# Two 128x2 helpers of a softmax on GpSimd instead of ScalarE

## The chip, the cores and the metric

The kernel runs on one core of one Trainium2 chip. The metric is the device time of one execution in microseconds; the figure before the change is the median of three runs. The core's engines are named as in the profile: PE is TensorE, DVE is VectorE, ACT is ScalarE, POOL is GpSimd, SP is SyncE, which issues most DMAs. PEld is PE's weight load, which overlaps its matmuls.

## The reference

Attention over 4 batches, 8 heads, 768 rows and head size 64, in which a query sees only keys with the same six-bit hash, and then a feed-forward layer over all 3072 rows:

```python
q_bits = (np.einsum('bhsd,dk->bhsk', q, proj) > 0)      # k_bits likewise
mask = q_bucket[:, :, :, None] == k_bucket[:, :, None, :]
scores = scale * np.matmul(q, k.transpose(0, 1, 3, 2))
scores = np.where(mask, scores, -1000000000.0)
scores = scores - np.max(scores, axis=-1, keepdims=True)
attn = np.exp(scores)
attn = attn / (np.sum(attn, axis=-1, keepdims=True) + 1e-09)
out = np.matmul(attn, v)
...
h = x @ w_in                                            # 3072x512 by 512x2048
g = np.where(h > 0.0, h, np.exp(np.minimum(h, 0.0)) - 1.0)
return g @ w_out                                        # 2048x512
```

## The kernel before, in words

All matmuls run in fp16 with every operand split in a high part (hi) and the rest (lo), so that three products of halves give near-fp32 results. Splitting a tile takes two instructions: the high part, mostly on ACT (L142), and scale and subtract, mostly on DVE (L151, one SCALAR_TENSOR_TENSOR that reads the tile and its high part). For the low parts of the weights and of half of the first V tiles, POOL does it in two steps (L153 scales in place, L154 subtracts).

The 3072 rows are cut in eight chunks of 384 (four batches, two each). A chunk has four pairs of heads; a pair of heads has six score rows of 128 queries by 768 keys, called slots here: 24 slots a chunk, 192 in all. What happens in a slot:

- `scores` (L556): four matmuls make a 128x768 score row in PSUM (tile s, or so in every second slot of the opening). DVE's L568 clamps it, copies it to SBUF as pt, and leaves the row maximum in one column of m. This frees the PSUM tile for the next slot.
- After every second slot, `exps` is traced for the two rows (a duo in the code, a pair of score rows in the text): L581 makes nb, the negated and scaled maximum, 128x2; L584 takes the exponential of each row with nb as bias, and leaves the row sum in a column of sm.
- One slot later, `splits`: L593 makes r from sm (scaled, with 1e-9 added), 128x2; DVE's L594 takes the reciprocal; then each row is split in halves (hl, ACT L142 and DVE L151) and transposed by an SP-issued DMA into PT (L599).
- Four slots after the last row of a pair of heads, `attend` multiplies PT with V (L607), and the result is split to x (L616 on ACT, L617 on DVE).

Beside this runs the feed-forward layer of an earlier chunk, 16 tiles of 128 hidden columns a chunk: `h` matmuls (L636), exponential on ACT (L647), `e*up + dn` on POOL (L650), select on DVE (L651), split (ACT L142, DVE L151, tiles U), and two or three tiles later the `o` matmuls (L672). After 16 tiles three output tiles are scaled and written by POOL-issued DMAs (L686).

The opening, up to some 170 us, loads and decodes the weights (L516 on ACT, L517 and L518 on DVE), measures them on PE (L526, tile acc), and splits them (tiles W with scales w0s and w1s), while the first chunk's attention runs. Other names: natk, nat1q and nat2q are split K and Q, zb the hash bits (L320), qm to sg small 128x2 factors, sg holding the scale of the scores and its negative.

A scheduler in the tile framework orders the instructions of each engine by its own estimate of their durations, and sets the semaphores. From slot 30 on (the start of the feed-forward part) PE's order is kept as traced; ACT, DVE, POOL and SP are always ordered by the scheduler. Each engine runs its queue in order.

Of the kernel before, what the change touches and what calls it, by code (L numbers as in the profile page):

```python
# [13 lines left out]
AF = mybir.ActivationFunctionType  # L14
ALU = mybir.AluOpType
# [7 lines left out]
P_TOP = 14  # L23
# [42 lines left out]
def lsh_attention_moe(  # L66
# [10 lines left out]
    nc = tc.nc  # L77
# [60 lines left out]
    def scaled(kind, o, x, s):  # L138

        e = engine(kind)  # L140
        if e == "A":
            nc.scalar.activation(o, x, AF.Copy, scale=s)  # L142
        elif e == "V":
            nc.vector.tensor_scalar(o, x, s, None, ALU.mult)
        else:
            nc.gpsimd.tensor_scalar(o, x, s, 1.0, ALU.mult, ALU.mult)

    def rest(kind, o, x, s, hi):

        if engine(kind) == "V":  # L150
            nc.vector.scalar_tensor_tensor(o, x, s, hi, ALU.mult, ALU.subtract)  # L151
        else:
            nc.gpsimd.tensor_scalar(x, x, s, 1.0, ALU.mult, ALU.mult)  # L153
            nc.gpsimd.tensor_tensor(o, x, hi, ALU.subtract)  # L154
# [421 lines left out]
    def exps(st, duo):  # L576

        m, pts = duo[0], duo[1:]
        w = len(pts)
        nb = small.tile([P, 2], F32, tag="nb", name="nb")  # L580
        nc.scalar.activation(nb[:, :w], m[:, :w], AF.Copy, scale=st["sg"][:, 1:2])  # L581
        sm = small.tile([P, 2], F32, tag="sm", name="sm")
        for n, pt in enumerate(pts):
            nc.scalar.activation(  # L584
                pt, pt, AF.Exp, bias=nb[:, n : n + 1], scale=st["sg"][:, 0:1], accum_out=sm[:, n : n + 1]
            )
        return sm, pts

    def splits(sm, pts, PTs):

        w = len(pts)
        r = small.tile([P, 2], F32, tag="r", name="r")
        nc.scalar.activation(r[:, :w], sm[:, :w], AF.Copy, scale=2.0**-P_TOP, bias=1e-9 * 2.0**-P_TOP)  # L593
        nc.vector.reciprocal(r[:, :w], r[:, :w])  # L594
        for n, pt in enumerate(pts):
            hl = pp.tile([P, 2, S], F16, tag="p", name="hl")
            scaled("p_hi", hl[:, 0, :], pt, r[:, n : n + 1])
            rest("p_lo", hl[:, 1, :], pt, r[:, n : n + 1], hl[:, 0, :])
            nc.sync.dma_start_transpose(PTs[n].rearrange("p x c e -> p (x c) e"), hl.rearrange("p x e -> p (x e)"))  # L599
# [189 lines left out]
    for ns in groups:  # L789
# [3 lines left out]
        for n in ns:  # L793
            at = lead[2] if early else begin[n] - PREP[2]

            w = 2 * chunks[pairs[n][0]]["nc"]
# [144 lines left out]
    def run_splits():  # L941
        if behind:
            splits(*behind.pop())

    for G in range(starts[-2] + 1):
        if G == starts[0]:
            ordered.enter_context(tc.manual_schedule(engines={mybir.EngineType.PE}))
        if G < len(slots):
            n, at = slots[G]
            c = chunks[pairs[n][0]]  # L950
            b, p, j, t = c["b"], pairs[n][1], at // c["nc"], at % c["nc"]
            now[0] = int(w_at == NSI + NSO)
            if t == 0:
                (PT,) = pt_ring.take(c["nc"], pairs[n][0])
                PTs = PTs + [PT] if j else [PT]
            if G < starts[0] and G % 2:
                s_tile = ps_o.tile([P, 2, 512], F32, tag="o", name="so")
            else:
                s_tile = ps_s.tile([P, 2, 512], F32, tag="s", name="s")
            scores(ks[b, p], qs[n], at, j, s_tile, duo, G >= starts[0])  # L960
            into.append(PT[:, t])

            run_splits()
            if len(into) == 2:
                behind.append((*exps(qs[n], duo), into))
                duo, into = [], []
            if at == 2 * c["nc"] - 1:
                assert not into
                waiting.append((G + AV_LAG, (n, PTs)))
        else:  # L970
            run_splits()
# [39 lines left out]
```

## Time and profile before

| | |
|---|---|
| median of three runs | 927.86 us (924.74 to 927.88) |
| the profiled execution | 925.77 us, span of its instructions 923.3 us |
| mean granted PE clock | 0.938 of full speed |
| busy: PE, DVE, ACT, POOL | 823.7, 698.3, 696.0, 221.9 us |
| PE busy, 0 to 184 us / 184 to 876 us | 109.2 / 675.1 us |

The page cuts the span in 40 slices; a digit is a busy share in tenths (9 is 90% or more), and PEclk the granted clock in tenths.

```profile
PE   4475745899999999999989999999999999999996
DVE  6999968788878778788868687889878687674332
ACT  7876878989869677789879677888687777774322
POOL 1703579631112011212211111221111112111211
PEclk9577656899999999999999999999999999999998
```

The first eight slices are the opening, in which PE has gaps and a lower granted clock. From the ninth on PE is nearly always busy, and in the last four no attention is left.

A row of a group has the line, engine and operation, the output and inputs, shapes and count, then the busy time and the mean in ns of one, and then the idle time before and what ended it. A row of the timeline has its start and its duration in us. A row of waits has who waited for whom, the total in us, the count and the longest.

### The profile page before, as it was taken

The numbers are of one execution on the slowest core, as the hardware profiler recorded it, in microseconds if no ns is written. First come the engines' busy times: TensorE is split into PE (matmuls) and PEld (weight loads), VectorE is DVE, ScalarE is ACT, GpSimd is POOL, SyncE is SP. The second block draws the span as 40 slices with busy tenths as digits, with TensorE's granted clock in tenths as the row PEclk, the third lists the DMA queues.
The fourth block names the chain that finished last, engine by engine and source line by source line (L and its number), as shares of the span: only waits on it lengthen the run. The fifth ranks groups of instructions, "written<-read, shape, count | busy, mean of one in ns | idle before, by whom it ended". The sixth has DMA issues, their size and how long they took to land.

```text
span 923.3 us, 14935 instructions
## 1 busy us (share of the span) xinstructions
PE 823.7 (89%) x5161; PEld 434.4 (47%) x5161; DVE 698.3 (76%) x1490; ACT 696.0 (75%) x1361; POOL 221.9 (24%) x259
## 2 busy tenths in 40 slices
PE   4475745899999999999989999999999999999996
PEld 2232312455545555555545555555445555555553
DVE  6999968788878778788868687889878687674332
ACT  7876878989869677789879677888687777774322
POOL 1703579631112011212211111221111112111211
PEclk9577656899999999999999999999999999999998
DMA  9799576798787857698897776896876678554000
GB/s 327 202 282 254 143 148 128 138 170 174 154 177 160 144 111 142 146 191 141 154 216 130 129 127 120 165 192 110 158 140 130 118 118 151 100 108 84 35 1 34
DMA packets 391338, 135.11 MB, mean 146 GB/s; under 512 B 368000, under 2 KB 385632, under 8 KB 391264
## 3 DMA queue, kind: packets, MB, share of 16 engines
q1 hardware_dynamic: 389184, 127.88, 69.3%
q0 software_dynamic: 1920, 6.29, 2.0%
q8 instruction: 40, 0.66, 0.3%
q14 instruction: 34, 0.28, 0.1%
q10 hardware_dynamic: 160, 0.00, 0.0%
HBM read 35.65 MB, written 6.29 MB: 45 GB/s over the span
## 4 chain that ended last, share of the span: by engine, by line
PE 45%; DVE 19%; DMA 13%; ACT 12%; issue 8%; POOL 1%; SPq 1%; ACTq 0%; POOLq 0%; DVEq 0%
PE h L636 16%; PE o L672 15%; PE s L556 7%; PE av L607 6%; DVE pt L568 5%; DVE hl L151 4%; DMA K<-natk 4%; ACT pt L584 3%; DMA O<-nat1q 3%; ACT hl L142 3%; DMA PT<-hl 2%; DMA out_dram<-W 2%; DVE W L518 1%; ACT U L647 1%; PE z L315 1%
## 5 line engine op out<-in xcount | busy, mean ns | idle before, releaser
L672 PE MATMUL o<-W,U 128*128 128x512 f16 x1152 | 280.9, 380 | 2.4 <-ACT W L142 2.4
L636 PE MATMUL h<-x,W 128*128 128x384 f16 x1536 | 280.5, 327 | 2.6 <-DVE x L617 2.2
L650 POOL TENSOR_SCALAR U<-U,ch 128x384 f32<-128x384 f32 x128 | 113.4, 886 | 572.1 <-ACT U L647 506.0
L636 PEld LDWEIGHTS <-W 128*128 128x128 f16 x1536 | 147.5, 98 | 114.1 <-issue 10.7
L151 DVE SCALAR_TENSOR_TENSOR hl<-pt,r,hl 128x768 f16<-128x768 f32 x192 | 193.9, 1038 | 6.3 <-ACT hl L142 5.9
L584 ACT ACTIVATE pt<-pt,nb,sg 128x768 f32<-128x768 f32 x192 | 195.3, 1018 | 2.2
L142 ACT ACTIVATE hl<-pt,r 128x768 f16<-128x768 f32 x192 | 168.4, 925 | 29.8 <-DVE r L594 27.6
L568 DVE TENSOR_SCALAR_CACHE_REDUCE pt<-s 128x768 f32<-128x768 f32 x177 | 168.0, 949 | 25.1 <-PE s L556 24.4
L556 PE MATMUL s<-K,O 128*128 128x384 f16 x708 | 151.5, 337 | 22.7 <-DVE pt L568 19.8
L672 PEld LDWEIGHTS <-U 128*128 128x128 f16 x1152 | 111.1, 98 | 122.3 <-issue 8.8
L556 PEld LDWEIGHTS <-O 128*128 128x128 f16 (+1 forms) x768 | 74.8, 102 | 115.6 <-issue 59.2
L651 DVE SCALAR_TENSOR_TENSOR U<-h,U 128x384 f32<-128x384 f32 x128 | 70.8, 553 | 74.8 <-POOL U L650 74.7
L647 ACT ACTIVATE U<-h,ch 128x384 f32<-128x384 f32 x128 | 72.8, 569 | 66.2 <-PE h L636 66.1
L607 PE MATMUL av<-PT,vhl 128*64 128x384 f16 x1152 | 106.9, 332 | 3.8 <-DMA PT<-hl 3.7
L151 DVE SCALAR_TENSOR_TENSOR U<-U,ch 128x384 f16<-128x384 f32 x128 | 79.6, 623 | 39.7 <-ACT U L142 39.4
L142 ACT ACTIVATE U<-U,ch 128x384 f16<-128x384 f32 x128 | 77.2, 605 | 40.8 <-DVE U L651 40.5
L607 PEld LDWEIGHTS <-vhl 128*64 128x64 f16 x1152 | 68.8, 111 | 44.4 <-issue 15.4
L154 POOL TENSOR_TENSOR W<-W 128x512 f16<-128x512 f32 x32 | 43.5, 1363 | 2.2
L581 ACT ACTIVATE nb<-m,sg 128x2 f32<-128x2 f32 x96 | 27.5, 287 | 16.4 <-DVE pt L568 15.9
L584 ACT ACTIVATION_READ_ACCUMULATOR pt<-pt,nb,sg 128x1 f32 x192 | 36.0, 187 | 0.0
L526 PE MATMUL acc<-W 128*128 128x128 bf16 x128 | 17.8, 283 | 19.7 <-DVE W L518 19.2
L556 PE MATMUL so<-K,O 128*128 128x384 f16 (+1 forms) x60 | 18.7, 449 | 17.9 <-DVE pt L568 16.6
(126 smaller groups left out, 632.5 us busy)
## 6 DMA issues: line engine op xcount, KB each, us to landing
U<-in_moe_w_in_dram SPq DMA_DIRECT2D x12, 512.0 KB
vf<-in_v_dram SPq DMA_DIRECT2D x16, 384.0 KB
U<-in_moe_w_out_dram SPq DMA_DIRECT2D x12, 512.0 KB
out_dram<-W POOLq DMA_DIRECT2D x24, 256.0 KB, 3.4
qst<-in_q_dram SPq DMA_DIRECT2D x30, 192.0 KB
kst<-in_k_dram SPq DMA_DIRECT2D x14, 384.0 KB
PT<-hl SPq DMA_TRANSPOSE x192
W<-in_moe_w_in_dram SPq DMA_DIRECT2D x4, 512.0 KB
```

The lines of the kernel that those rows point to most:

```text
L142: nc.scalar.activation(o, x, AF.Copy, scale=s)
L151: nc.vector.scalar_tensor_tensor(o, x, s, hi, ALU.mult, ALU.subtract)
L154: nc.gpsimd.tensor_tensor(o, x, hi, ALU.subtract)
L556: nc.tensor.matmul(s_tile[:, n, :HALF], st[o][:rows, at, :], kst[kk][:rows, j * NC + n * HC : j * NC + (n + 1) * HC, :].rearrange("p a b - ...
L568: top = nc.vector.tensor_scalar(pt.rearrange("p (n e) -> p n e", n=2), s_tile[:, :, :HALF], CLAMP, None, ALU.max, ALU.max, accum_out=duo[0 ...
L584: nc.scalar.activation(pt, pt, AF.Exp, bias=nb[:, n : n + 1], scale=st["sg"][:, 0:1], accum_out=sm[:, n : n + 1])
L607: nc.tensor.matmul(av[j * D : (j + 1) * D], vt[:, j, c, vx, :], PTs[j][:, :, px, c, :], start=n == 0, stop=n == last,)
L636: nc.tensor.matmul(h, WH[:, g * KT + t, wx, fc * P : (fc + 1) * P], c["xs"][t][:, xx, :], start=n == 0, stop=n == 3 * KT - 1,)
L647: nc.scalar.activation(e, h, AF.Exp, scale=c["ch"])
L650: nc.gpsimd.tensor_scalar(e, e, c["up"], c["dn"], ALU.mult, ALU.add)
L651: nc.vector.scalar_tensor_tensor(e, h, 0.0, e, ALU.max, ALU.min)
L672: nc.tensor.matmul(o[t][:, :DO], g16[:, gx, t * P : (t + 1) * P], WH[:, NSI + 1 + f, wx, :], start=f == 0 and i == 0, stop=f == NF - 1 and ...
```

## The change

L581 and L593, the two 128x2 instructions between the row maxima and the exponentials and between the row sums and the reciprocal, are issued on POOL instead of ACT. nb reads one operand per partition (sg) and an immediate 1.0; r has two immediates. Nothing else is edited; the scheduler orders the changed program anew.

```diff
         nb = small.tile([P, 2], F32, tag="nb", name="nb")
-        nc.scalar.activation(nb[:, :w], m[:, :w], AF.Copy, scale=st["sg"][:, 1:2])
+        nc.gpsimd.tensor_scalar(nb[:, :w], m[:, :w], st["sg"][:, 1:2], 1.0, ALU.mult, ALU.mult)
...
         r = small.tile([P, 2], F32, tag="r", name="r")
-        nc.scalar.activation(r[:, :w], sm[:, :w], AF.Copy, scale=2.0**-P_TOP, bias=1e-9 * 2.0**-P_TOP)
+        nc.gpsimd.tensor_scalar(r[:, :w], sm[:, :w], 2.0**-P_TOP, 1e-9 * 2.0**-P_TOP, ALU.mult, ALU.add)
         nc.vector.reciprocal(r[:, :w], r[:, :w])
```

Three places of the new order are shown in the prediction: POOL between two output DMAs, where 96 nb and 96 r now stand among the 128 L650; DVE behind a row maximum; and POOL among the weight splits of the opening.

## The prediction

> **What bounds the kernel now.** I read the page's busy shares first, then busy time by stretch, then the waits of PE, and last single rows in order of time. The columns of the second view are the stretch, its length, busy time of PE, PE's weight loads, DVE, ACT and POOL, then granted PE clock, DMA share and GB/s.
>
> ```profile
> PE 823.7 (89%) x5161; PEld 434.4 (47%) x5161; DVE 698.3 (76%) x1490; ACT 696.0 (75%) x1361; POOL 221.9 (24%) x259
> 23.00:115.00 92.00, 57.28 (x347) 29.46 (x346) 89.56 (x199) 73.02 (x137) 38.10 (x30) 0.65 0.85 221
> 115.00:184.00 69.00, 42.64 (x229) 19.64 (x229) 51.90 (x93) 59.07 (x116) 53.11 (x51) 0.70 0.73 138
> 184.00:876.00 692.00, 675.07 (x4318) 359.82 (x4317) 529.87 (x1124) 534.07 (x1055) 120.01 (x141) 1.00 0.74 140
> ```
>
> There are two kernels in one. From 184 us on, PE is busy 675.07 of 692.00 us, and only 16.9 us can be won there. Before that no engine is full all the time: DVE has 97% of 23 to 115 us, and from 115 to 184 us ACT has 86%, POOL 77%, DVE 75%. POOL does 91 of its 222 us between 23 and 184 us; later it is busy 17%.
>
> What PE still waits for after 184 us:
>
> ```profile
> PE s L556 <- DVE pt L568: 10.5, 10, 2.3
> PE o L672 <- ACT W L142: 2.4, 4, 1.2
> PE av L607 <- DMA PT<-hl: 2.4, 4, 1.1
> ```
>
> The largest wait is for the row maximum (L568), which empties the one score tile in PSUM. So a delay counts there only when it makes a later L568 late, or the transposed probabilities (PT).
>
> **The change, part by part.** *Removed from ACT:* 96 of each instruction (the third and fourth row are the stretches up to 167 and from 23 to 115 us).
>
> ```profile
> L581 ACT ACTIVATE nb<-m,sg 128x2 f32<-128x2 f32 x96 | 27.5, 287 | 16.4 <-DVE pt L568 15.9
> L593 ACT ACTIVATE r<-sm 128x2 f32<-128x2 f32 x96 | 18.3, 190 | 0.2
> L581 ACT ACTIVATE nb<-m,sg x14: 278/281/297, 24.4 to 162.2; 128x2 f32<-128x2 f32 x14
> L581 ACT ACTIVATE nb<-m,sg x8: 278/281/297, 24.4 to 106.8; 128x2 f32<-128x2 f32 x8
> 50.98 0.28 ACT L581 ACTIVATE nb<-m,sg 128x2 f32<-128x2 f32 x1
> 51.17 0.65 ACT L516 ACTIVATE W<-W 128x512 f32<-128x512 f32 x1
> 90.61 0.19 ACT L593 ACTIVATE r<-sm 128x2 f32<-128x2 f32 x1
> 90.70 0.66 ACT L516 ACTIVATE W<-U 128x512 f32<-128x512 f32 x1
> ```
>
> Busy time is 27.5 + 18.3 = 45.8 us, but the next instruction starts 0.19 us after an nb and 0.09 us after an r, since neighbours overlap. ACT really gets back 0.28 us per pair of score rows: 27 us over 96 pairs. 14 pairs lie before 167 us (3.9 us), 82 after it. Before 115 us DVE is the full engine, so I count half of the 3.9: −2 us. Behind 184 us ACT is busy 77% and PE's waits name it with 2.4 us: −1 us.
>
> *Added on POOL, busy time:* no 128x2 TENSOR_SCALAR runs on POOL before the change, so its price comes from the shortest of wider ones (columns: min/median/max in ns) and, as a floor, from a memset of one column.
>
> ```profile
> L153 POOL TENSOR_SCALAR vf<-vf,vs x8: 582/945/1532, 29.2 to 42.9; 128x384 f32<-128x384 f32 x8
> L153 POOL TENSOR_SCALAR W<-W,w1s x16: 687/698/1659, 115.0 to 188.2; 128x512 f32<-128x512 f32 x16
> L650 POOL TENSOR_SCALAR U<-U,ch x128: 652/666/2766, 172.9 to 910.4; 128x384 f32<-128x384 f32 x128
> L237 POOL MEMSET pjt<- 32x1 f32 x8 | 0.5, 91 | 0.2
> ```
>
> 128 more columns cost 105 ns, 0.82 ns each, so 384 columns are 315 ns and the fixed part is 267 ns with one operand read per partition (nb's form). L650 reads two and has 337 ns, so one such operand is 70 ns, and r, with none, would be near 197 ns. The sum is 0.46 us per pair, 45 us in all. The low end is 0.18 us (two memsets of 91 ns), the high end 1.33 us (two of L650's median, as if width cost nothing); I take 0.46, worked out from the same kind of instruction. Behind 184 us POOL has 572 us idle, which hides it; if POOL were full, those 82 pairs would cost 38 us.
>
> *Hops.* Here is one pair in the steady part, in order of time.
>
> ```profile
> 307.84 1.01 DVE L151 SCALAR_TENSOR_TENSOR hl<-pt,r,hl 128x768 f16<-128x768 f32 x1
> 307.96 0.29 ACT L581 ACTIVATE nb<-m,sg 128x2 f32<-128x2 f32 x1 [0.63 <-DVE pt L568]
> 308.28 1.03 ACT L584 ACTIVATE pt<-pt,nb,sg 128x768 f32<-128x768 f32 x1
> 308.77 0.61 DVE L151 SCALAR_TENSOR_TENSOR U<-U,ch 128x384 f16<-128x384 f32 x1
> 310.32 0.56 ACT L647 ACTIVATE U<-h,ch 128x384 f32<-128x384 f32 x1
> 310.98 0.67 POOL L650 TENSOR_SCALAR U<-U,ch 128x384 f32<-128x384 f32 x1 [5.49 <-ACT r L593]
> 311.68 0.56 DVE L651 SCALAR_TENSOR_TENSOR U<-h,U 128x384 f32<-128x384 f32 x1 [0.51 <-POOL U L650]
> 312.27 0.61 ACT L142 ACTIVATE U<-U,ch 128x384 f16<-128x384 f32 x1 [1.30 <-DVE U L651]
> 312.92 0.62 DVE L151 SCALAR_TENSOR_TENSOR U<-U,ch 128x384 f16<-128x384 f32 x1 [0.68 <-ACT U L142]
> 313.45 0.95 DVE L568 TENSOR_SCALAR_CACHE_REDUCE pt<-s 128x768 f32<-128x768 f32 x1
> 314.33 0.08 DVE L568 DVE_READ_ACCUMULATOR pt<-s 128x1 f32 x1
> 315.17 0.82 PE L556 MATMUL s<-K,O 128*128 128x384 f16 x4
> ```
>
> L647 ends at 310.88 and POOL starts at 310.98: a hop to POOL is 0.10 us. POOL ends at 311.65, DVE starts at 311.68: 0.03 us back. Undisturbed, nb costs 0.10 + 0.27 + 0.03 = 0.40 us on its path against 308.28 − 307.92 = 0.36 us now, and r about 0.10 us more than now. By that the move would be nearly free in latency.
>
> *Disturbance by DVE.* It isn't undisturbed. This L650 fell into a run of DVE's L151:
>
> ```profile
> 257.82 1.94 DVE L151 SCALAR_TENSOR_TENSOR hl<-pt,r,hl 128x768 f16<-128x768 f32 x2
> 257.99 2.76 POOL L650 TENSOR_SCALAR U<-U,ch 128x384 f32<-128x384 f32 x1 [4.57 <-ACT U L647]
> 259.68 0.60 DVE L151 SCALAR_TENSOR_TENSOR U<-U,ch 128x384 f16<-128x384 f32 x1
> ```
>
> It took 2.76 us where the median is 0.67, and ended 0.47 us after the third L151. L151 reads two tensors from SBUF. So POOL stands still until a run of them is over. The Trainium skill says why: in "SBUF — State Buffer", section "SBUF: two separate sides", the port pair that DVE and GpSimd share is an exclusive lock, taken for a whole instruction by a DVE operation with two SBUF inputs or by a GpSimd one, and the other blocks. The row agrees; by that rule nothing of such a wait is shared or shortened, and the sum below would stand at its upper end for every nb that meets one.
>
> How often does nb meet it? It is released by the second L568 of a pair, so what DVE has in its queue right behind that decides. In the changed order that is an L151 in 41 of 96 pairs. DVE in the fourth of eight chunks, before (pt is the score row, m its maximum, hl the split probabilities, U a feed-forward tile, natk the split K, zb the hash bits):
>
> ```order
> L151 SCALAR_TENSOR_TENSOR natk<-kst,ks,natk 128x768
> L568 TENSOR_SCALAR pt,m<-s 128x768
> L651 SCALAR_TENSOR_TENSOR U<-h,U 128x384
> L151 SCALAR_TENSOR_TENSOR hl<-pt,r,hl 128x768
> L320 TENSOR_SCALAR zb<-z,pjt 64x384
> L151 SCALAR_TENSOR_TENSOR hl<-pt,r,hl 128x768
> ```
>
> and DVE at the same place now:
>
> ```order
> L151 SCALAR_TENSOR_TENSOR natk<-kst,ks,natk 128x768
> L568 TENSOR_SCALAR pt,m<-s 128x768
> L151 SCALAR_TENSOR_TENSOR hl<-pt,r,hl 128x768 x2
> L320 TENSOR_SCALAR zb<-z,pjt 64x384
> L651 SCALAR_TENSOR_TENSOR U<-h,U 128x384
> ```
>
> The two hl splits moved ahead of L651, straight behind the maximum that releases nb. One L151 holds POOL for 1.01 us, two for 1.94; 1.2 us is my mean.
>
> In the pair quoted above L151 starts at 307.84, nb could start at 307.92 + 0.10 = 308.02 at the earliest and would wait for both L151, until 309.38. With its 0.27 and the hop, the exponentials (L584) would start at 309.68 instead of 308.28, 1.4 us late. L647 follows them on ACT, L650, L651, the next U split and then L568 follow that one by one, each released by the last or nearly so; L568 would end 1.4 us later than 314.41, at 315.8, where PE wants the tile at 315.17. PE loses 0.6 us. Where ACT has idle time between, it loses nothing. Blocked pairs in the steady part: 82 × 41/96 = 35. At 0.6 us each this is 21 us, the upper end; the lower is 0. I let somewhat under half of it through: +9 us. In the opening 14 × 41/96 = 6 pairs are blocked; 1.2 us each, half of it kept because ACT is idle 14 to 21% there: +3 us (0 to 7).
>
> *What queues behind on POOL.* POOL is in order, so L650 and the weight splits now stand behind an nb that waits for DVE and an r that waits for ACT. POOL in the steady part, before:
>
> ```order
> L650 TENSOR_SCALAR U<-U,ch 128x384 x15
> L686 DMA out_dram<-W 128x512 x2
> L650 TENSOR_SCALAR U<-U,ch 128x384
> L686 DMA out_dram<-W 128x512
> L650 TENSOR_SCALAR U<-U,ch 128x384 x15
> ```
>
> and now, behind the second chunk's output:
>
> ```order
> L650 TENSOR_SCALAR U<-U,ch 128x384
> L686 DMA out_dram<-W 128x512
> L581 TENSOR_SCALAR nb<-m,sg 128x2
> L650 TENSOR_SCALAR U<-U,ch 128x384
> L593 TENSOR_SCALAR r<-sm 128x2
> ```
>
> Where fifteen L650 followed each other, an nb or an r now stands between two of them. DVE's L651 waits for L650, PE's o matmuls come two feed-forward tiles later, and PE waits only 2.4 us for all outputs: I cost this at nothing there. The cover is that lag of two tiles; if it is gone, each late L650 stops PE's o matmul. SP's queue loses and gains no DMA.
>
> *DVE held by POOL.* It goes the other way too: of the 192 L151 of this form the median took 1010 ns and the longest 1904.
>
> ```profile
> L151 DVE SCALAR_TENSOR_TENSOR hl<-pt,r,hl x192: 998/1010/1904, 34.8 to 839.0; 128x768 f16<-128x768 f32 x192
> ```
>
> On the full DVE of 23 to 115 us some 8 pairs × 0.46 = 3.7 us is the most that small POOL operations can take; they must start first to do so: +1 us.
>
> Sum: −2 − 1 + 9 + 3 + 1 = +10 us. The profiled execution took 925.77 us (span 923.3), so 935.8, told as 936. It lies 2.1 us under the median of the runs, 927.86.
>
> **Rivals.** *ACT's time is worth more (faster).* The freed 27 us shorten ACT's queue, hl and U splits come earlier, L568 is never late. For it: undisturbed latency is the same within 0.1 us, and most L650 run at 0.67 us. Against it: only 17 us of PE waits exist behind 184 us and ACT is not full there. The whole 3.9 us of the opening and half of the 10.5 us on L568 go: 925.77 − 9 = 917. It decides if nb's mean stays below about 0.5 us.
>
> *All hidden (no change).* Blocked nb are covered by ACT's 23% idle time, the freed 0.28 us pays for the rest: 926 to 930. For it: PE is 97.6% busy and loses only 2.4 us to PT today. Against it: the pair above, where every step followed at once.
>
> *POOL and ACT chain each other in the opening (much slower).* From 115 to 184 us POOL is busy 77% with weight splits, and ACT's next high part overwrites what POOL's low part reads. There POOL has, before (w0s and w1s are the scales of the two weights):
>
> ```order
> L153 TENSOR_SCALAR W<-W,w1s 128x512
> L154 TENSOR_TENSOR W<-W 128x512
> L153 TENSOR_SCALAR W<-W,w0s 128x512
> L153 TENSOR_SCALAR W<-W,w1s 128x512
> L154 TENSOR_TENSOR W<-W 128x512 x2
> ```
>
> and now:
>
> ```order
> L153 TENSOR_SCALAR W<-W,w1s 128x512
> L581 TENSOR_SCALAR nb<-m,sg 128x2
> L154 TENSOR_TENSOR W<-W 128x512
> L153 TENSOR_SCALAR W<-W,w0s 128x512
> L154 TENSOR_TENSOR W<-W 128x512
> L593 TENSOR_SCALAR r<-sm 128x2
> ```
>
> The scaling (L153) and the subtraction (L154) of one weight tile are parted by an nb, and an r that waits for exponentials holds the next tile. 14 − 8 = 6 pairs, two holds each, each as long as one row's exponentials (1.03 + 0.19 us): +15 us on the forecast, 951. Against it: ACT waits little for POOL there now:
>
> ```profile
> ACT W L142 <- POOL W L154: 1.2, 4, 0.6
> ```
>
> **How the numbers follow.** Something under 0.5% (4.6 us) can't be told from no change. Blocked nb, as summed: 0.45, of which 0.41 beyond 932.5 us and 0.04 within; its own range is 929 to 950, from the nb terms' ends. All hidden: 0.28. ACT's time worth more: 0.15. The chain in the opening: 0.12. So faster 0.15, same 0.32, slower 0.53. The range leaves out the better half of the faster case (0.08) and, at the top, the chain with longer holds (some 0.06): 922 to 955.
>
> **What would show it.** Right: nb on POOL with a median near 0.3 us but a mean above 0.6 and a maximum above 1.5; DVE's and ACT's idle time in the steady part up; PE's wait for L568 behind 184 us above 10.5 us, towards 20; the first feed-forward matmul (L636) later than the 166.91 us of this row:
>
> ```profile
> 166.91 1.63 PE L636 MATMUL h<-x,W 128*128 128x384 f16 x9
> ```
>
> Wrong: nb's mean below 0.5 us, or PE's waits unchanged despite long nb (the 9 us fall away), or an opening that ends earlier because the changed order of ACT and DVE there happens to fit better, which I can't price from the trace.

## The result and the profile after

The changed kernel takes 939.35 us (median of four runs, 935.04 to 943.29) against 926.30 of the kernel before, timed beside it on the same chip: 1.0139 times as long, 95% interval 1.0117 to 1.0161, or 13 us. The profiled execution took 937.45 us, with a span of 935.7; before it was 925.77 and 923.3.

Busy time over the whole span, from the page:

```profile
PE 828.0 (88%) x5161; PEld 434.7 (46%) x5161; DVE 703.1 (75%) x1490; ACT 663.3 (71%) x1169; POOL 293.0 (31%) x451
```

And the three stretches of before (stretch, length, busy us of PE, PE's weight loads, DVE, ACT and POOL, granted PE clock, DMA share, GB/s):

```profile
23.00:115.00 92.00, 50.59 (x305) 26.18 (x305) 85.70 (x188) 70.42 (x119) 41.05 (x44) 0.63 0.82 222
115.00:184.00 69.00, 47.29 (x245) 22.58 (x244) 49.04 (x96) 53.30 (x93) 58.25 (x63) 0.71 0.71 128
184.00:876.00 692.00, 668.71 (x4275) 353.68 (x4276) 539.21 (x1128) 507.38 (x902) 181.13 (x303) 1.00 0.74 141
```

ACT has 33 us less to do and POOL 71 us more, yet PE does 6.4 us less of its work between 184 and 876 us (668.71 against 675.07). Besides PE (97%) no engine is full: DVE is busy 78% there, ACT 73%, POOL 26%. So the loss is to be looked for in waits. PE's, from 184 us on (who waited for whom, total us, count, longest):

```profile
PE s L556 <- DVE pt L568: 17.1, 16, 2.5
PE av L607 <- DMA PT<-hl: 2.1, 3, 0.9
```

The wait for the row maximum grew from 10.5 to 17.1 us; the one for the transposed probabilities did not. One engine further back, the groups of the moved instructions and their neighbours (busy us, mean ns of one | idle before it and what ended it):

```profile
L581 POOL TENSOR_SCALAR nb<-m,sg 128x2 f32<-128x2 f32 x96 | 56.0, 583 | 235.5 <-DVE pt L568 159.0 <-DVE qm L187 31.9 <-DVE qs L200 21.4
L593 POOL TENSOR_SCALAR r<-sm 128x2 f32<-128x2 f32 x96 | 22.4, 233 | 159.7 <-ACT pt L584 158.7
L584 ACT ACTIVATE pt<-pt,nb,sg 128x768 f32<-128x768 f32 x192 | 195.4, 1019 | 79.3 <-POOL nb L581 79.0
```

The same wait by the view of waits, ACT from 190 to 900 us:

```profile
ACT pt L584 <- POOL nb L581: 71.4, 61, 3.2
```

The exponentials are as long as before (1019 ns against 1018), but ACT, whose queue is in order, now stands idle 79.0 us in front of them. In the kernel before it stood 16.4 us in front of its own nb, as quoted in the prediction. So ACT lost more to waiting than the 45.8 us of busy time it was relieved of. Part of such a wait is for the maximum itself: counting only the time between the end of a pair's second maximum and its first exponential, over the 81 pairs behind the opening, ACT is idle 56.4 us now and was 11.3 us before. How long nb and r take, minimum, median and maximum in ns:

```profile
L581 POOL TENSOR_SCALAR nb<-m,sg x96: 254/267/2298, 25.3 to 845.4; 128x2 f32<-128x2 f32 x96
L593 POOL TENSOR_SCALAR r<-sm x96: 181/191/1482, 28.0 to 847.9; 128x2 f32<-128x2 f32 x96
```

The medians are small. The mean of nb is more than twice its median, since a third of them are stretched. One of these, from the opening, with the rows of DVE around it in order of time:

```profile
158.83 1.01 DVE L151 SCALAR_TENSOR_TENSOR hl<-pt,r,hl 128x768 f16<-128x768 f32 x1
...
159.00 1.42 POOL L581 TENSOR_SCALAR nb<-m,sg 128x2 f32<-128x2 f32 x1 [0.49 <-DVE pt L568]
...
159.76 0.60 DVE L151 SCALAR_TENSOR_TENSOR nat2q<-qst,qs,nat1q 128x384 f16<-128x384 f32 x1
...
160.46 1.03 ACT L584 ACTIVATE pt<-pt,nb,sg 128x768 f32<-128x768 f32 x1 [3.12 <-POOL nb L581]
```

nb is released at 159.00, but two L151 run until 160.36, and it ends 0.06 us after them; the exponential starts 0.04 us later. ACT had been idle for 3.12 us, about half of it before the maximum was there. The first feed-forward matmul comes 3.9 us later than before:

```profile
170.81 2.44 PE L636 MATMUL h<-x,W 128*128 128x384 f16 x14
```

### The profile page after: what moved, and what is told of

Its sections match the earlier page's. It is cut to its first block, busy times and chain, and to the rows that moved or that the text cites. A ratio compares the mean times of both kernels' runs of the same rounds, so it can differ in the third digit from the quotient of the medians.

```text
span 935.7 us, 15092 instructions
## 1 busy us (share of the span) xinstructions
PE 828.0 (88%) x5161; PEld 434.7 (46%) x5161; DVE 703.1 (75%) x1490; ACT 663.3 (71%) x1169; POOL 293.0 (31%) x451
## 5 line engine op out<-in xcount | busy, mean ns | idle before, releaser
L636 PE MATMUL h<-x,W 128*128 128x384 f16 x1536 | 281.0, 327 | 0.0
L584 ACT ACTIVATE pt<-pt,nb,sg 128x768 f32<-128x768 f32 x192 | 195.4, 1019 | 79.3 <-POOL nb L581 79.0
L151 DVE SCALAR_TENSOR_TENSOR hl<-pt,r,hl 128x768 f16<-128x768 f32 x192 | 195.1, 1047 | 9.0 <-ACT hl L142 8.7
L636 PEld LDWEIGHTS <-W 128*128 128x128 f16 x1536 | 147.8, 98 | 111.7 <-issue 10.9
L568 DVE TENSOR_SCALAR_CACHE_REDUCE pt<-s 128x768 f32<-128x768 f32 x177 | 168.3, 951 | 16.0 <-PE s L556 15.0
L650 POOL TENSOR_SCALAR U<-U,ch 128x384 f32<-128x384 f32 x128 | 112.3, 878 | 202.1 <-ACT U L647 190.8
L581 POOL TENSOR_SCALAR nb<-m,sg 128x2 f32<-128x2 f32 x96 | 56.0, 583 | 235.5 <-DVE pt L568 159.0
L607 PE MATMUL av<-PT,vhl 128*64 128x384 f16 x1152 | 108.8, 339 | 6.4 <-DMA PT<-hl 5.6
L151 DVE SCALAR_TENSOR_TENSOR U<-U,ch 128x384 f16<-128x384 f32 x128 | 79.6, 622 | 21.6 <-ACT U L142 19.5
L593 POOL TENSOR_SCALAR r<-sm 128x2 f32<-128x2 f32 x96 | 22.4, 233 | 159.7 <-ACT pt L584 158.7
L594 DVE RECIPROCAL r<-r 128x2 f32<-128x2 f32 x96 | 15.7, 163 | 59.0 <-POOL r L593 58.7
```

Of the source, the lines that this page charges most:

```text
L568: top = nc.vector.tensor_scalar(pt.rearrange("p (n e) -> p n e", n=2), s_tile[:, :, :HALF], CLAMP, None, ALU.max, ALU.max, accum_out=duo[0 ...
L581: nc.gpsimd.tensor_scalar(nb[:, :w], m[:, :w], st["sg"][:, 1:2], 1.0, ALU.mult, ALU.mult)
L584: nc.scalar.activation(pt, pt, AF.Exp, bias=nb[:, n : n + 1], scale=st["sg"][:, 0:1], accum_out=sm[:, n : n + 1])
L607: nc.tensor.matmul(av[j * D : (j + 1) * D], vt[:, j, c, vx, :], PTs[j][:, :, px, c, :], start=n == 0, stop=n == last,)
L636: nc.tensor.matmul(h, WH[:, g * KT + t, wx, fc * P : (fc + 1) * P], c["xs"][t][:, xx, :], start=n == 0, stop=n == 3 * KT - 1,)
L650: nc.gpsimd.tensor_scalar(e, e, c["up"], c["dn"], ALU.mult, ALU.add)
```

## The experiments

Each kernel was timed against the kernel before on the same chip, whose medians lay between 924.83 and 925.60 us (926.30 for the change itself). Where us are given as a gain or loss, they are differences of the medians of one chip. The right part of the table is from the profiled executions: how much later than before the 43rd and the last of the 192 slots started (the L568 rows in order; the 43rd starts at 219.5 us before), how long ACT was held up for nb between 190 and 900 us, and the median time from the end of a pair's second row maximum to the start of its first exponential, over the 81 pairs behind the opening.

| | median us | ratio, 95% interval | slot 43 | slot 192 | ACT idle for nb, us | max to exp, median us |
|---|---|---|---|---|---|---|
| before | | 1 | | | 15.0 | 0.58 |
| the change | 939.35 | 1.0139 (1.0117 to 1.0161) | +8.9 | +12.6 | 71.4 | 1.10 |
| nb alone on POOL | 940.94 | 1.0169 (1.0151 to 1.0187) | +3.1 | +16.4 | 64.8 | 1.10 |
| r alone on POOL | 927.34 | 1.0023 (1.0012 to 1.0033) | +5.6 | +1.8 | 30.4 | 0.51 |
| both on POOL, opening only | 930.25 | 1.0051 (1.0033 to 1.0068) | +5.9 | +5.0 | 14.5 | 0.60 |
| both on POOL, from slot 30 on | 935.72 | 1.0114 (1.0095 to 1.0132) | +5.1 | +10.3 | 72.4 | 1.10 |
| both on DVE | 933.27 | 1.0081 (1.0061 to 1.0101) | +2.8 | +8.4 | 51.0 | 1.63 |
| nb alone on DVE | 934.11 | 1.0093 (1.0079 to 1.0106) | +4.0 | +9.3 | 38.9 | 1.66 |
| both on ACT, unused copies on POOL | 932.79 | 1.0080 (1.0062 to 1.0098) | +6.7 | +7.0 | 15.7 | 0.65 |
| nb on POOL in two steps | 961.35 | 1.0386 (1.0367 to 1.0405) | +11.7 | +37.5 | 82.6 | 1.69 |
| nb on ACT in two steps | 942.18 | 1.0165 (1.0143 to 1.0186) | +6.5 | +16.8 | 9.3 | 1.33 |
| unused copy of sm on ACT | 928.51 | 1.0033 (1.0011 to 1.0055) | −0.6 | +1.2 | 14.4 | 0.73 |

The start of slot 43 scatters by a few us from kernel to kernel, and no run separates why, so single numbers of that column carry little; the growth from slot 43 to slot 192 is steadier. That growth goes with the last column: the seven kernels in which the median is above 1 us lose between 3.7 and 25.8 us behind slot 43, the four others at most 1.8. Its size does not follow the median: nb alone on DVE, at 1.66 us, loses 5.3 there, and nb in two steps on POOL, at 1.69, loses 25.8. ACT's idle time for nb alone is no measure of the loss either: with r alone on POOL it is twice that of before, and with nb on ACT in two steps it is less.

**Which of the two.** nb alone on POOL:

```diff
-        nc.scalar.activation(nb[:, :w], m[:, :w], AF.Copy, scale=st["sg"][:, 1:2])
+        nc.gpsimd.tensor_scalar(nb[:, :w], m[:, :w], st["sg"][:, 1:2], 1.0, ALU.mult, ALU.mult)
```

> Only nb (L581) goes to POOL; r stays on ACT. Whole change: +1.39% (+13 us). Theory A, nb blocked behind DVE's L151 makes the exponentials late: most of it returns, +8 to +12 us, nb's mean near 0.58 us and its maximum above 2 us, ACT waiting some 70 us for nb. Theory B, POOL's queue and the two-way chain with ACT in the opening: nb and r share it, +4 to +8 us. Theory C, the scheduler's new order of ACT and DVE: anything from -5 to +13 us, with no relation to nb's duration.

And r alone:

```diff
-        nc.scalar.activation(r[:, :w], sm[:, :w], AF.Copy, scale=2.0**-P_TOP, bias=1e-9 * 2.0**-P_TOP)
+        nc.gpsimd.tensor_scalar(r[:, :w], sm[:, :w], 2.0**-P_TOP, 1e-9 * 2.0**-P_TOP, ALU.mult, ALU.add)
```

> Only r (L593) goes to POOL; nb stays on ACT. Theory A: r is released by ACT, not by DVE's row maximum, so it seldom meets a run of L151; mean near 0.23 us, and the time is within 3 us of before. Theory B: +4 to +8 us, since r holds the weight splits on POOL until the exponentials are done. Theory C: anything from -5 to +13 us.

nb alone costs 15.5 us, all that the change costs and a little more; r alone 1.9 us. With nb on POOL the lag grows from +3.1 us at slot 43 to +16.4 at the end; with r it shrinks. r's wait is behind the exponentials and one slot ahead of the split that uses it. nb's stands between the row maximum and the exponentials, with ACT waiting. The 15.5 us lie above all three ranges, 3.5 us above theory A's; its other signs came (nb's mean is 609 ns, ACT idle for nb 64.8 us). For r, theory A's range of 3 us held. PE's waits with nb alone on POOL, from 184 us on, show a second way of the loss: beside the row maximum, PE now waits for the transposed probabilities, which cost it 2.4 us before.

```profile
PE s L556 <- DVE pt L568: 17.4, 18, 2.7
PE av L607 <- DMA PT<-hl: 8.9, 9, 1.8
```

The pair of kernels also bears on theory C, the new order. If the instructions of ACT and DVE are matched by operation and tiles, without the moved helpers, then r alone has 188 of ACT's 913 and 375 of DVE's 1298 out of the order of before (the fewest that would have to be moved back), the whole change 181 and 365, and nb alone 129 and 190. As much re-ordering as in the change comes with 1.9 us, less of it with 15.5. So the amount of re-ordering is not what costs; that one particular order does is not excluded by this.

**Which part of the run.** The two new lines are chosen by a flag that is set at slot 30 (here the opening; the other kernel has the branches exchanged):

```diff
-        nc.scalar.activation(nb[:, :w], m[:, :w], AF.Copy, scale=st["sg"][:, 1:2])
+        if not late[0]:
+            nc.gpsimd.tensor_scalar(nb[:, :w], m[:, :w], st["sg"][:, 1:2], 1.0, ALU.mult, ALU.mult)
+        else:
+            nc.scalar.activation(nb[:, :w], m[:, :w], AF.Copy, scale=st["sg"][:, 1:2])
...
+        late[0] = int(G >= starts[0])
```

> nb and r on POOL only for the pairs of score rows before slot 30, on ACT after it. In the profile after, slot 30 began 5.2 us and slot 42 8.9 us later than before, the last slots 12.6 us later. Theory A: the opening has 15 pairs, some 6 blocked, +3 to +5 us at slot 30 and no more after it. Theory B: +8 to +10 us, all of it by slot 42. Theory C: the opening's order is that of the changed kernel, so slot 30 is late by the same 5 us whatever POOL does.

> nb and r on POOL only from slot 30 on, on ACT before it. Theory A: 81 pairs, some 35 blocked: +5 to +9 us, spread evenly over the slots, with PE's wait for L568 after 184 us at 15 to 18 us. Theory B: the weight splits still run until slot 36 or so: +2 to +5 us, all of it between slots 30 and 42. Theory C: with the opening as before, -3 to +5 us.

+4.8 us for the opening, +10.3 for the steady part; together 15.0 against 13.0 for the whole change, within the intervals. The opening's loss is complete by slot 43 and does not grow; at slot 31 it is 4.3 us, which fits theories A and C alike. The steady part's loss is not spread evenly, as theory A had it: 5.1 of the 10.3 us are there by slot 43, 3.6 of them from slot 31 on, where theory B had its loss; the other 5.2 come behind it. PE's wait for L568 is 16.6 us, within theory A's 15 to 18. The changed kernel itself has lost 5.2 us by slot 31, 8.9 by slot 43, and 3.7 us behind that.

**Without POOL.** If the block of POOL by L151 were all of it, nb on DVE would be nearly free:

```diff
-        nc.scalar.activation(nb[:, :w], m[:, :w], AF.Copy, scale=st["sg"][:, 1:2])
+        nc.vector.tensor_scalar(nb[:, :w], m[:, :w], st["sg"][:, 1:2], None, ALU.mult)
```

> nb and r go to DVE instead of POOL: ACT is freed by the same instructions, but nothing stands on POOL and nothing has to wait there. nb only on POOL cost +1.69% (15.6 us), all of it after slot 30. Theory A, the wait of nb for a run of L151 and the late exponentials behind it: without POOL the loss is gone, 920 to 928 us (DVE pays some 0.15 us for each, of which a few us may show in the opening, where DVE is full). Theory C, the order that the scheduler makes when ACT has less to do: the loss stays, 934 to 942 us. Theory D, the load taken off ACT and put elsewhere is what counts: ACT had 77% and DVE 77% in the steady part, so the time stays within 3 us of before.

> Only nb goes to DVE, r stays on ACT. Theory A: 920 to 928 us, against 941 with nb on POOL. Theory C: 934 us or more. If both this and the kernel with both on DVE are faster than before, nb's place is what the gain belongs to.

Theory A missed on both: 933.27 and 934.11 us, not 920 to 928. Theory C's 934 or more, for the order of the scheduler, is met with nb alone and missed by 0.7 us with both. With nb alone on DVE it is short (min/median/max in ns):

```profile
L581 DVE TENSOR_SCALAR nb<-m,sg x96: 210/223/1203, 25.6 to 842.0; 128x2 f32<-128x2 f32 x96
```

And yet ACT waits for it, here by the view of waits from 190 to 900 us:

```profile
ACT pt L584 <- DVE nb L581: 38.9, 39, 1.8
```

In the order of that kernel an L151 stands straight ahead of nb on DVE in 61 of the 96 pairs. So there nb waits in DVE's queue for the same kind of instruction that held it on POOL. The delay has another cause and the same place, and the kernel loses 8.5 us. These two kernels do not part lateness from order: that an L151 stands ahead of nb is itself the scheduler's order.

**Without the path.** nb and r are made on ACT as before, and POOL makes both a second time into tiles that nobody reads:

```diff
+        nbx = small.tile([P, 2], F32, tag="nx", name="nbx", bufs=1)
+        nc.gpsimd.tensor_scalar(nbx[:, :w], m[:, :w], st["sg"][:, 1:2], 1.0, ALU.mult, ALU.mult)
...
+        rx = small.tile([P, 2], F32, tag="nx", name="rx", bufs=1)
+        nc.gpsimd.tensor_scalar(rx[:, :w], sm[:, :w], 2.0**-P_TOP, 1e-9 * 2.0**-P_TOP, ALU.mult, ALU.add)
```

> nb and r stay on ACT and are used from there; POOL makes the same two 128x2 results a second time, into a tile that nobody reads. Theory A: nobody waits for these, so 0 to +4 us, although they last as long on POOL as in the changed kernel. Theory B, POOL's queue (L650 and the weight splits behind waiting instructions) and DVE held by POOL: the same +6 to +13 us as the change.

It loses 7.2 us, above theory A's 4 and within theory B's 6 to 13, all of it by slot 43. Behind that, POOL has the same small instructions in its queue, stretched the same way, and nothing is lost. Their group, with a mean of 591 ns:

```profile
L583 POOL TENSOR_SCALAR nbx<-m,sg 128x2 f32<-128x2 f32 x96 | 56.7, 591 | 185.1 <-DVE pt L568 108.3 <-DVE qm L187 41.5 <-DVE qs L200 21.5
```

In the opening ACT waits for POOL's low parts of the weights (0 to 190 us). It was 1.2 us in the kernel before; in this one it is:

```profile
ACT W L142 <- POOL W L154: 6.0, 6, 2.2
```

In the changed kernel that wait is 4.9 us, with both on POOL in the opening only 6.4. It is of the size of the opening's loss. Order has little part in it here: counted as above, only 17 instructions of ACT and 11 of DVE stand elsewhere than before, all between 133 and 195 us. The lag grows from 1.0 us at slot 29 (161 us) to 6.5 at slot 34 (182 us), while POOL splits weights. So a loss as large as the opening's arises without a late nb; how it divides between POOL's queue, DVE held by POOL and the few moved instructions is open.

**The dose.** nb alone on POOL, with a second instruction behind it:

```diff
+        nc.gpsimd.tensor_scalar(nb[:, :w], nb[:, :w], 1.0, 1.0, ALU.mult, ALU.mult)
```

> As nb only on POOL (940.9 us), and a second 128x2 instruction on POOL multiplies nb by 1 before ACT may use it: some 0.2 to 0.3 us more on the path of each pair, and a second chance to meet an L151. Theory A, the time follows nb's lateness (0.3 us more on average cost 15.6 us): +5 to +15 us on top, 946 to 956 us. Theory C, order alone: within 4 us of 941.

The group of that second instruction:

```profile
L582 POOL TENSOR_SCALAR nb<-nb 128x2 f32<-128x2 f32 x96 | 49.1, 511 | 6.7
```

PE's wait for the row maximum, 184 to 930 us:

```profile
PE s L556 <- DVE pt L568: 31.3, 31, 2.0
```

49.1 us more between maximum and exponentials cost 20.3 us more than nb alone on POOL (35.8 against 15.5), and PE's wait is three times that of before. Of the lag added to that of nb alone, 8.6 us are there by slot 43 and 12.5 follow over the rest. The direction is theory A's; its range ended at 15 us, and 961.35 lies 5 us above it.

**One operand of L151 in PSUM.** To see whether the two SBUF inputs of L151 are what holds POOL, the high part that DVE's splits subtract was replaced by a zero in PSUM:

```diff
+    av_bank = ps_a.tile([P, 512], F32, tag="av", name="av")
+    zero_ps = av_bank[:, 448:452]
...
-            nc.vector.scalar_tensor_tensor(o, x, s, hi, ALU.mult, ALU.subtract)
+            nc.vector.scalar_tensor_tensor(o, x, s, z, ALU.mult, ALU.subtract)
```

where z is one column of zero_ps, repeated, and av takes the rest of the same bank. The second kernel has nb on POOL besides.

> The kernel before (nb and r on ACT) with one operand of every DVE split of the form L151 taken from PSUM instead of SBUF: the high part that is subtracted is replaced by a zero in an unused corner of the PSUM bank of av. It leaves out the subtraction of the high part, and keeps the wait for it. It is the base for the next run, and has its own order of DVE. Theory lock (POOL stands still while DVE reads two operands from SBUF): POOL's L650 no longer stretches, maximum below 1.2 us where it was 2.77, and the time is 915 to 930. Theory order (an engine other than ACT makes nb late by its place in a queue, the lock is a small part): L650's maximum may fall as well, the time is 920 to 935. If L650 still stretches past 2 us, two operands in SBUF are not what holds POOL.

> The run above with nb alone on POOL. It too leaves out the subtraction of the high part. To be compared with the run above, as nb alone on POOL (940.94) is with the kernel before (925.47), +15.5 us. Theory lock: nb has a mean of 0.27 to 0.32 us and no instance above 0.7, and the difference falls to +4 us or less. Theory order: nb is as short as that, but ACT still waits 40 us or more for it, and the difference stays at +8 us or more, as when nb ran on DVE (+8.6).

The times were 1364.62 and 1387.42 us (ratios 1.4733, 1.4701 to 1.4765, and 1.4975, 1.4933 to 1.5018), far from both expectations. Since av and the zero share a tile, the matmuls that write to this tile wait until DVE has read the zero. PE's largest such wait in the first kernel, from 190 us on:

```profile
PE av L329 <- DVE U L161: 155.9, 38, 8.8
```

The difference between the two, 22.8 us, is as theory order had it (8 or more), and so is ACT's idle time for nb, 54.1 us; but in the first kernel, with nb on ACT, that time is already 49.3 us. The difference is one of a kernel that waits elsewhere, and it decides nothing about the time. The durations do decide something. L151 is line 161 here, L650 line 664 and nb line 595. In the first kernel, L151 as a group (busy us, mean ns) and by min/median/max, and L650 by min/median/max:

```profile
L161 DVE SCALAR_TENSOR_TENSOR hl<-pt,r,av 128x768 f16<-128x768 f32 x192 | 186.9, 1009 | 38.6 <-ACT hl L147 38.6
```

```profile
L161 DVE SCALAR_TENSOR_TENSOR hl<-pt,r,av x192: 998/1009/1015, 35.1 to 1278.0; 128x768 f16<-128x768 f32 x192
```

```profile
L664 POOL TENSOR_SCALAR U<-U,ch x128: 652/664/696, 182.1 to 1352.0; 128x384 f32<-128x384 f32 x128
```

nb in the second kernel, by both views:

```profile
L595 POOL TENSOR_SCALAR nb<-m,sg 128x2 f32<-128x2 f32 x96 | 26.7, 278 | 498.8 <-DVE pt L582 342.8 <-DVE qm L201 142.1 <-DVE w0e L209 13.4
```

```profile
L595 POOL TENSOR_SCALAR nb<-m,sg x96: 259/263/1002, 26.5 to 1290.9; 128x2 f32<-128x2 f32 x96
```

L650's longest fell from 2766 to 696 ns with the median unchanged (664 and 666), and nb's from 2298 to 1002, its mean from 583 to 278. DVE's split has the same median as before (1009 and 1010), and its own longest fell from 1904 to 1015 ns: the hold is gone both ways. Nor did L650 merely miss the splits in a longer kernel: before, 39 of the 128 ran beside an L151 for more than 0.2 us, and the longest of these is the one of 2766 ns; in the first kernel 46 do, and the longest of these takes 666 ns. So it is the second SBUF input that holds POOL. The expectation of no nb above 0.7 us was missed by two, 970 and 1002 ns; both ran beside L532, which decodes weights and still reads two tensors from SBUF, here the longer one:

```profile
82.82 1.00 POOL L595 TENSOR_SCALAR nb<-m,sg 128x2 f32<-128x2 f32 x1 [13.42 <-DVE w0e L209]
82.95 0.67 DVE L532 SCALAR_TENSOR_TENSOR W<-U,W 128x512 int32<-128x512 int32 x1
```

The Trainium skill, "SBUF — State Buffer", section "SBUF: two separate sides", says that such an instruction takes the port pair shared with GpSimd for its whole length, and that the other blocks. The rows of L650 agree: 2766 ns with two operands in SBUF, 696 with one.

**Late, or busy?** Two kernels without POOL and DVE in the matter. One makes nb on ACT in two steps, the other adds an instruction of about the same length on ACT that nobody waits for:

```diff
         nc.scalar.activation(nb[:, :w], m[:, :w], AF.Copy, scale=st["sg"][:, 1:2])
+        nc.scalar.activation(nb[:, :w], nb[:, :w], AF.Copy, scale=1.0)
```

> The kernel before with a second ACT instruction that multiplies nb by 1 in place: nb is 0.19 to 0.28 us later and ACT has 15 to 20 us more to do behind 184 us, POOL and DVE have nothing more. Theory lock: without POOL in the path little happens, +0 to +4 us, 926 to 930. Theory lateness (each nb that is later delays the slot, whatever makes it late; the second instruction on POOL cost 20 us): +8 us or more, 934 or above.

```diff
+        smx = small.tile([P, 2], F32, tag="nx", name="smx", bufs=1)
+        nc.scalar.activation(smx[:, :w], sm[:, :w], AF.Copy, scale=1.0)
         return sm, pts
```

> The kernel before with one more 128x2 instruction on ACT for each pair of score rows that nobody waits for: it scales the row sums sm by 1 into an unused tile, traced behind both exponentials. ACT gets the same 0.2 us per pair more to do as when nb was made in two ACT instructions (942.18, +16.9), but not between a row maximum and an exponential. Theory lateness (what delays nb delays the slot): clearly less than that, +0 to +7 us, 925 to 933, the upper end since unused copies on POOL cost 7 by re-ordering the opening. Theory ACT time (0.2 us on ACT are worth about 0.17 us of time wherever they stand): +12 to +18 us, 937 to 944.

The added group in the first kernel:

```profile
L582 ACT ACTIVATE nb<-nb 128x2 f32<-128x2 f32 x96 | 19.1, 199 | 1.9
```

And in the second:

```profile
L588 ACT ACTIVATE smx<-sm 128x2 f32<-128x2 f32 x96 | 18.3, 191 | 0.2
```

For the same 0.2 us of ACT per pair, one loses 16.9 us (942.18 against 925.29) and the other 3.7 (928.51 against 924.83). What was edited differs in the place and in what waits for it: between the row maximum and the exponentials, or behind them. That tells lateness from ACT's load, and from POOL and the lock: no POOL operation was added in either. It does not tell it from order, since the scheduler ordered both anew, the first by more (140 and 223 instructions of ACT and DVE out of place, against 55 and 84). In the profiled executions the two differ by 7.1 us at slot 43 and by 15.6 at the last, so 8.5 us arise behind the opening. Here too PE's wait for PT grew, to 8.2 us, beside that for L568, 14.6.

## Why the prediction was right

The forecast was 936 us, range 922 to 955, slower by over 0.5% at 0.53; the measured 939.35 lies in it and is slower by 1.39%. The main mechanism was right: an nb on POOL that meets DVE's L151 is stretched, the exponentials wait for it, and PE waits longer for L568. That the time came within 4 us is in part luck, since several terms were off in opposite directions. By its steps:

- *Price on POOL.* 0.267 and 0.197 us were worked out from the widths of other TENSOR_SCALARs; the medians are 267 and 191 ns. The sum of 45 us became 78.4 (56.0 + 22.4), since the stretch, which the prediction counted on its own, is in it. The floor of 0.18 us and the ceiling of 1.33 were far.
- *Disturbance by DVE.* Right in kind. A mean above 0.6 us was named as the sign and is just missed, with 0.583; the maximum is 2.298, above the 1.5 named. Both halves of the term were off in opposite directions: counted from the rows behind 167 us, 28 of 82 nb took over 0.5 us (35 forecast), and the stretch over 0.267 us sums to 24.7 us (35 × 1.2 = 42 forecast); but a larger part of it was let through, if the 10.3 us of the kernel with the change from slot 30 on are put down to it (10.3 of 24.7, against 9 of 42). The forecast had 9 − 1 us for the steady part. That these come near each other is luck; the changed kernel's own lag grows by 7.4 us behind slot 31.
- *What the term left out.* It tied the whole loss to L151's hold on POOL. nb on DVE (+8.5 us) and nb in two steps on ACT (+16.9 us) show that a delay between row maximum and exponentials costs on other engines too. The price is not uniform: nb in two steps on ACT against the unused copy gives 16.9 − 3.7 = 13.2 us for 19.1 us of busy time there, 0.69 per us; the second step on POOL 20.3 for 49.1, 0.41 per us. nb's busy time rose by 56.0 − 27.5 = 28.5 us, which by these two is an estimate of 12 to 20 us, against 13.0 measured. It is a rough one, since busy time is not the delay: nb on DVE is busy 27.0 us, no more than on ACT, and its kernel loses 8.5 us, with an L151 ahead of nb in most pairs.
- *ACT freed: −3 us.* Not confirmed. 18.3 us more of busy time on ACT off the path cost 3.7 us, with an interval of 1.0 to 5.1; by that price the 45.8 us of busy time taken off would be worth some 9 us, an estimate, three times the 3 forecast and as much as the rival of a faster kernel gave it. No run only takes load off ACT. The rival fails on its other condition: nb's mean is 0.583 us, not below 0.5, and L568 is later, not earlier. If the freed time is worth more than 3 us, the delay costs more than the sum shows.
- *POOL's queue, nothing in the steady part.* Right: the unused copies lose nothing behind slot 43. *In the opening* that queue was left to a rival of 0.12 with +15 us; the wait that it names is there, at a quarter of that size: ACT's wait for POOL's weight splits, 1.2 us before, is 4.9 us. The opening costs 4.8 us instead of the +2 that the sum came to (3 for blocked nb, 1 for DVE, less 2), so this part was mis-sized. The unused copies lose 6.7 us by slot 43 with nb on ACT, so blocked nb need not be what the opening pays for.
- *DVE held by POOL: +1 us.* By the groups the 192 hl splits take 195.1 us, 193.9 before, and the 30 of nat2q 20.5 instead of 19.0: +2.7 us in all, so the size was near, though its path was not tried.
- *The chain to PE.* PE's wait for L568 was to rise towards 20 us: 17.1. L636 was to start later: by 3.9 us. The forecast of more idle time held for ACT alone; DVE is busy 9.3 us more in the steady stretch. It is busy 6.7 us less in the two stretches before, so most of this is work that came later.

Open is how the loss in the steady part divides between the stretch by L151 and the hand-over from DVE to POOL to ACT: the kernels made to part them, with an operand in PSUM, stalled on av. The delay is seen in the median from the end of the second row maximum to the first exponential, 0.58 us before and 1.10 after, but not in the mean, 1.22 and 1.10, over the 81 pairs behind the opening. Before, 16 of the pairs waited over 2 us, after, 10 do; but before, ACT mostly ran other work in that time and was idle for 11.3 of 98.8 us, after, for 56.4 of 89.3. That ACT's later work, the high parts that DVE's queue waits for, is what then makes L568 and PT late fits this, but was not followed slot by slot. And no run held the scheduler's order fixed behind the opening while nb was late, so the share of order in each single number is open.

## What to carry to other kernels

A tiny instruction is priced by the wait that it sits in, not by its own length: 0.2 us per pair cost 16.9 us between the maximum and the exponentials and 3.7 us behind them, on the same engine. Before moving work off an in-order engine, compare the time that is freed in its queue with the time that it will then stand idle for the result: here 27 us (46 us of busy time, which overlaps its neighbours) against 45 us more behind the row maximum. Such a comparison can give the direction; it did not give the size in these kernels. And a helper on GpSimd that is released by VectorE meets whatever VectorE runs next; look in VectorE's queue for an instruction with two SBUF inputs there, before moving it.

## What the runs showed of the hardware

That a DVE instruction with two SBUF inputs holds GpSimd was forecast. One operand from PSUM lifts the hold: in 128 L650 the longest is 696 ns against 2766, with the same median of DVE's instruction (1009 and 1010 ns), whose own longest fell from 1904 to 1015. A GpSimd instruction is held over the whole run of such DVE instructions, not for one: 1.42 us for nb in the rows shown, through two L151. A GpSimd TENSOR_SCALAR on 128x2 had a median of 267 ns with one operand per partition and of 191 ns with two immediates, against means of 287 and 190 ns on ACT and a median of 223 ns for nb on DVE: the three engines differ by some 0.1 us in it, and in these kernels that decided little.
